# Attention scores in three rounded products from the first pair, an earlier end of the interleaved order, and later front loads

## The chip, the cores and the metric

The kernel runs on one core of a Trainium2 chip. The metric is the time of one execution in microseconds on the device, the median of several runs. The engines are TensorE (PE; PEld are its weight loads), VectorE (DVE), ScalarE (ACT), GpSimd (POOL) and the DMA queues that SyncE (SP) and ScalarE issue.

## What is computed

Block-causal attention over 8 batches, 8 heads, 576 positions of 64 features, and a gated two-layer network on its output.

```python
scores = (1 / sqrt(D)) * q @ k.T              # B, H = 8, 8; S = 576; D = 64
scores = where(row // 64 >= col // 64, scores, -1e9)
attn = softmax(scores)                        # per row, + 1e-9 in the denominator
x = (attn @ v).transpose(0, 2, 1, 3).reshape(4608, 512)
out = (sigmoid(x @ w_gate) * (x @ w_val)) @ w_out    # w_gate, w_val: 512 x 1536, w_out: 1536 x 512
```

Inputs and output are float32, but for the three weight arrays, which arrive as 64-bit numbers and are converted on the chip.

## The kernel before

**Two halves.** The first half goes through 32 pairs of heads (4 pairs a batch): attention, and beside it a first third of the network (`mlp1`, hidden units 0 to 511) for the batch whose four pairs are done. The second half is the rest of the network. The change lies in the first half, roughly the first 580 us of the span.

**Precision.** A matmul takes float32 tiles as they are, in one product, or the kernel rounds a tile to the type F32R (high part H), keeps what rounding left as a second tile (low part L), and adds three products: H with H, L with H, H with L. The network does this throughout (`hidden`, `out_mm`). Attention scores did it only for pairs after `N_FIRST` = 7, and there not for the first 128 rows of q; those, and all scores of pairs 0 to 7, are one float32 product from the tile `KQ` (k and scaled q, transposed).

**A pair.** `prep(p)` makes the transposed tiles. For pairs 0 to 4 PE transposes the loaded rows (`rqk`, two buffers) into PSUM and ScalarE copies them to `KQ` (four copies: k and q, 512 and 64 columns). For pairs 5 to 7 DVE transposes and GpSimd scales q. For pairs 8 on, `split`: DVE transposes, ScalarE rounds K and Q into `KS[0]` and `QS[0]`, DVE subtracts into `KS[1]` and `QS[1]`, GpSimd scales the first 128 columns of q. `QB` holds the last 64 rows of q of both heads side by side for the tail scores. `attend(p)` gives the steps of the pair: "s3", "s2", "sl" (scores and softmax of row blocks 3, 2, and 1 with 0; "s" is all three), "t" (the tail, both heads together), "tr.." (transposes of the probabilities P on PE and their copies G by ScalarE), "r" (`recip`), "AV" (product with v, multiplied by `rb` on DVE, and the output to `X`).

**Reciprocals.** ScalarE sums each row while it computes exponentials, into a column of `sm`: columns 0 to 3 for head 0, 4 to 7 for head 1, column 8 for the tail of both heads (64 partitions each). `recip` inverts, transposes to `rT`, writes `rT` to DRAM (`r_d`, four transfers, L420), and reads it back spread over partitions (`rb`, four transfers, L424). All are on SP's queue.

**Order.** Each pair goes through a list of steps. `FIRST` interleaves the scores of pair p with the transposes of pair p - 1 (capitals: "TR2", "TRt", "TRl", "AV" are of the pair before); `REST` has all scores first and the transposes last; `TURN` is the list in between, for the one pair p = `N_FIRST`. "k" and "q" run `prep(p + 1)` one step further and load k and q of pair p + 3. The number beside a step is how many places it has for matmuls of `mlp1`, twelve a pair; they are dealt evenly (`rate`), tied behind PE instructions of the attention by order edges (`behind`), which also pin the scores in pairs after `N_FIRST` (`rest`, `hold`). Conversions of the weights (`convert`, L85 to L118; fetch on SP, then seven DVE and two ScalarE instructions a piece) are dealt over pairs 0 to 7 by `CONV_PLAN`: w_gate and w_val in pairs 0 to 6, w_out in pairs 5, 6 and 7; a fetch stands behind the last marked instruction of its queue, if there is one. The order on each engine is then fixed by a planner that issues whatever its own model says is ready, the earlier in the code first.

```python
FIRST = (("s3", 1), ("TR2", 1), ("k", 1), ("s2", 1), ("TRt", 1), ("q", 1), ("t", 1), ("TRl", 1), ("sl", 1), ("AV", 2),
         ("tr3", 1), ("r", 0))
REST = (("s", 3), ("t", 1), ("AV", 2), ("tr3", 1), ("r", 0), ("k", 0), ("tr2", 1), ("q", 0), ("trl", 2), ("trt", 2))
for what, places in (FIRST if p < N_FIRST else TURN if p == N_FIRST else REST):
```

The functions that the change touches:

Of the kernel before, what the change touches and what calls it, by code (L numbers as in the profile page):

```python
# [9 lines left out]
F32 = mybir.dt.float32  # L10
F32R = mybir.dt.float32r
# [19 lines left out]
         ("tr3", 1), ("r", 0))  # L31
REST = (("s", 3), ("t", 1), ("AV", 2), ("tr3", 1), ("r", 0), ("k", 0), ("tr2", 1), ("q", 0), ("trl", 2), ("trt", 2))
TURN = (("s3", 1), ("TR2", 1), ("k", 0), ("s2", 1), ("TRt", 1), ("q", 0), ("t", 1), ("TRl", 1), ("sl", 1), ("AV", 1),
        ("tr3", 1), ("r", 0), ("tr2", 1), ("trl", 1), ("trt", 1))
N_FIRST = 7
# [5 lines left out]
def attn_glu_kernel(ctx: ExitStack, tc: tile.TileContext, q, k, v, w_gate, w_val, w_out, out):  # L41
# [119 lines left out]
    with ExitStack() as s2:  # L161
# [9 lines left out]
        KS, QS = [at.tile([P, S], F32R, name=f"K{e}") for e in "HL"], [at.tile([P, S - P], F32R, name=f"Q{e}") for e in "HL"]  # L171
# [16 lines left out]

        QBs = [at.tile([P, 2, D], F32, name=f"QB{i}") for i in range(2)]
        QBS = [at.tile([P, 2, D], F32R, name=f"QB{e}") for e in "HL"]  # L190
        for QB in QBs + [x.bitcast(F32) for x in QBS]:
            nc.gpsimd.memset(QB, 0.0)
# [16 lines left out]
        def load(p, what, queue=nc.sync):  # L209
# [10 lines left out]
            if p <= NP:  # L220

                i, src = (0, k) if what == "k" else (1, q)
                r = rqks[p % 2].rearrange("p i s -> p (i s)").rearrange("p (t c) -> p t c", c=P)
                for h in range(2):
                    queue.dma_start(out=r[:, 4 * i:4 * i + 4, h * D:(h + 1) * D],
                                    in_=src[b, h0 + h, 0:4 * P, :].rearrange("(t p) d -> p t d", p=P))
                queue.dma_start(out=r[64 * i:64 * i + 64, 8, :].rearrange("p (h d) -> p h d", h=2),
                                in_=src[b, h0:h0 + 2, 4 * P:S, :].rearrange("h p d -> p h d"))
                return
# [11 lines left out]
        def mark(engine, ins):  # L241
            last[engine] = ins.ins
# [26 lines left out]
        def prep(p):  # L269

            split = p > N_FIRST
            KQ = cv.tile([P, 2, S], F32, name="KQ", bufs=2)
            QB = QBs[p % 2]

            def transposed(i):
                turn = last.get("DVE")
                mark("DVE", nc.vector.transpose(out=KQ[:, i], in_=rqks[p % 2][:, i]))
                if turn:
                    behind(last["DVE"], turn)

            if p <= NP:

                r = rqks[p % 2].rearrange("p i s -> p (i s)").rearrange("p (t c) -> p t c", c=P)

                def evict(dst, src, i):
                    if i:
                        mark("ACT", nc.scalar.mul(out=dst, in_=src, mul=scale))
                    else:
                        mark("ACT", nc.scalar.copy(out=dst, in_=src))

                for i in range(2):
                    pt = mbank()
                    for t in range(4):
                        transpose(pt[:, t * P:(t + 1) * P], r[:, 4 * i + t], ident)
                    evict(KQ[:, i, :4 * P], pt, i)
                    if i == 0:
                        yield
                pt = mbank()
                transpose(pt[:, :P], r[:, 8], ident)
                for i in range(2):  # L300
                    evict(KQ[:, i, 4 * P:], pt[:, 64 * i:64 * i + 64], i)
                for h in range(2):
                    nc.gpsimd.tensor_copy(out=QB[rows(h), h], in_=KQ[rows(h), 1, S - D:])
                if p == 0:
                    P_first.update({i: p_tile(i) for i in (3, 2, 1, 0, 4)})
                state[p] = KQ, QB, VSs[p % 3]
                yield
                return
            if split:
                transposed(0)  # L310
                transposed(1)
                mark("ACT", nc.scalar.copy(out=KS[0], in_=KQ[:, 0]))
                mark("ACT", nc.scalar.mul(out=QS[0], in_=KQ[:, 1, P:], mul=scale))
                nc.gpsimd.tensor_scalar_mul(KQ[:, 1, :P], KQ[:, 1, :P], scale)
                yield
                mark("DVE", nc.vector.tensor_sub(out=KS[1], in0=KQ[:, 0], in1=KS[0].bitcast(F32)))
                mark("DVE", nc.vector.scalar_tensor_tensor(out=QS[1], in0=KQ[:, 1, P:], scalar=scale,
                                                           in1=QS[0].bitcast(F32), op0=ALU.mult, op1=ALU.subtract))
                for x, src in zip(QBS, QS):
                    for h in range(2):  # L320
                        nc.gpsimd.tensor_copy(out=x[rows(h), h], in_=src[rows(h), S - P - D:])
                state[p] = KQ, QB, VSs[p % 3]
                yield
                return
            for i in range(2):
                transposed(i)
                if i == 1:
                    nc.gpsimd.tensor_scalar_mul(KQ[:, 1], KQ[:, 1], scale)
                    for h in range(2):
                        nc.gpsimd.tensor_copy(out=QB[rows(h), h], in_=KQ[rows(h), 1, S - D:])  # L330
                yield
            state[p] = KQ, QB, VSs[p % 3]

        def attend(p):
            b, hp = pairs[p]
            KQ, QB, VS = state.pop(p)
# [13 lines left out]
            def scores(ps, i, c):  # L350
# [4 lines left out]
                ops = [(KQ[:, 1, q], KQ[:, 0, :n])]  # L355
                if rest and i:
                    q = slice((i - 1) * P, i * P)
                    ops = [(QS[a][:, q], KS[b][:, :n]) for a, b in ((0, 0), (1, 0), (0, 1))]
# [7 lines left out]
            def softmax(ps, i, c):  # L366
# [5 lines left out]
                for h in range(2):  # L372
                    mark("ACT", nc.scalar.activation(out=Pi[:, h], in_=ps[:, h, c:c + n], func=AF.Exp,  # L373
                                                     bias=nm[:, c0 + h:c0 + h + 1], accum_out=sm[:, 4 * h + i:4 * h + i + 1]))
# [21 lines left out]
            def s_tail():  # L396
# [3 lines left out]
                ops = [(QBS[a], KS[b]) for a, b in ((0, 0), (1, 0), (0, 1))] if rest else [(QB, KQ[:, 0])]  # L400
                for half in range(2):
                    for k, (x, y) in enumerate(ops):
# [6 lines left out]
                                                 func=AF.Exp, bias=nm[:, c0:c0 + 1], accum_out=sm[:, 8:9]))  # L409

            def recip():
# [9 lines left out]
                for o, n, src in ((0, 4 * P, r_d[:8].rearrange("(h i) q -> h (i q)", h=2)),  # L421
                                  (4 * P, D, r_d[8].rearrange("(h q) -> h q", h=2))):
                    for h in range(2):
                        nc.sync.dma_start(out=rb[rows(h), o:o + n], in_=src[h].partition_broadcast(D))  # L424
# [328 lines left out]
        for p in range(n + 1):  # L753
# [4 lines left out]
            for what, places in (FIRST if p < N_FIRST else TURN if p == N_FIRST else REST):  # L758
# [8 lines left out]
                elif what in "kq":  # L767
                    next(pr, None)
                    for x in "kq":

                        if p + 3 < n and what == ("q" if p < NP else x):
                            load(p + 3, x)
                elif now:
                    now(what)
# [230 lines left out]
```

## Time and profile before

| | |
|---|---|
| median of three runs | 1217.52 us (1215.24 to 1217.72) |
| the profiled execution | 1215.93 us, span from first to last instruction 1214.1 us |
| PE busy | 1166.7 us, 96% of the span |
| PE weight loads | 1031.1 us, 85% |
| DVE, ACT, POOL busy | 771.9, 626.8, 333.7 us (64, 52, 27%) |
| chain of work that ended last | PE 76%, DVE 13%, DMA 4%, ACT 3% |

Busy PE time is modelled and matmuls overlap, so the distance between the starts of two instructions says more than the length of one. In the chain, a share is the part of the span in which that engine was what everything after it waited for. An average over the span hides that the first 150 us have other limits than the rest, so the stretches are read one by one.

### The profile page before, as it was taken

The numbers are of one execution on the slowest core, as the hardware profiler recorded it, in microseconds if no ns is written. First come the engines' busy times: TensorE is split into PE (matmuls) and PEld (weight loads), VectorE is DVE, ScalarE is ACT, GpSimd is POOL, SyncE is SP. The second block draws the span as 40 slices with busy tenths as digits, with TensorE's granted clock in tenths as the row PEclk, the third lists the DMA queues.
The fourth block names the chain that finished last, engine by engine and source line by source line (L and its number), as shares of the span: only waits on it lengthen the run. The fifth ranks groups of instructions, "written<-read, shape, count | busy, mean of one in ns | idle before, by whom it ended". The sixth has DMA issues, their size and how long they took to land.

```text
span 1214.1 us, 20793 instructions
## 1 busy us (share of the span) xinstructions
PE 1166.7 (96%) x7421; PEld 1031.1 (85%) x7421; DVE 771.9 (64%) x1447; ACT 626.8 (52%) x1447; POOL 333.7 (27%) x411
## 2 busy tenths in 40 slices
PE   6689899999999999999999999999999999999996
PEld 4457688888888888889798899999999998998995
DVE  5676955455463564545799977857867655745743
ACT  6676766666675766666434544444444422422420
POOL 0113232323332332313200133133032162361441
PEclk8899999999999999999999999999999999999998
DMA  8545343534435335444333345145187164263253
GB/s 211 136 120 110 94 113 71 127 67 105 109 79 129 80 85 117 90 103 113 105 106 130 109 148 200 42 159 193 35 307 279 65 201 141 69 208 131 78 156 104
DMA packets 251670, 152.51 MB, mean 126 GB/s; under 512 B 192048, under 2 KB 212528, under 8 KB 250928
## 3 DMA queue, kind: packets, MB, share of 16 engines
q1 hardware_dynamic: 240512, 132.02, 39.0%
q10 hardware_dynamic: 11056, 19.17, 4.4%
q8 instruction: 58, 0.95, 0.3%
q14 instruction: 44, 0.36, 0.1%
HBM read 103.81 MB, written 47.33 MB: 124 GB/s over the span
## 4 chain that ended last, share of the span: by engine, by line
PE 76%; DVE 13%; DMA 4%; ACT 3%; issue 2%; SPq 1%; POOL 1%; POOLq 0%; DVEq 0%; ACTq 0%
PE b L814 22%; PE m L126 14%; PE bank L245 13%; PE m L872 10%; PE m L135 6%; PE bank L248 6%; PE b L872 5%; DVE XL L706 2%; DMA pr<-part_d 1%; ACT P L373 1%; DVE nm L370 1%; DMA raw<-in_moe_w_val_dram 1%; DMA XB<-xT_d 1%; POOL pr L887 1%; DVE cT L616 1%
## 5 line engine op out<-in xcount | busy, mean ns | idle before, releaser
L814 PE MATMUL b<-XH,w 128*128 128x384 f32 x1344 | 351.2, 336 | 4.5 <-DVE g L850 2.0
L814 PEld LDWEIGHTS b<-XH,w 128*128 128x128 f32 x1344 | 244.6, 188 | 10.6 <-DVE v L850 4.5
L814 PE MATMUL b<-XL,w 128*128 128x384 f32 x672 | 225.2, 336 | 0.0
L373 ACT ACTIVATE P<-bank,nm 128x512 f32<-128x512 f32 (+3 forms) x256 | 133.4, 538 | 77.7 <-DVE nm L370 68.9
L814 PEld LDWEIGHTS b<-XL,w 128*128 128x128 f32 x672 | 126.5, 188 | 1.3
L872 PE MATMUL m<-wo,hH 128*128 128x512 f32 x384 | 125.2, 392 | 0.0
L370 DVE TENSOR_REDUCE nm<-bank 128x2 f32<-128x1024 f32 (+3 forms) x128 | 104.9, 820 | 31.4 <-ACT P L373 28.9
L348 ACT COPY G<-bank 128x768 f32<-128x768 f32 (+3 forms) x160 | 106.8, 697 | 34.7 <-PE bank L248 33.5
L126 PE MATMUL m<-XH,wg 128*128 128x288 f32 x448 | 106.3, 307 | 0.0
L126 PE MATMUL m<-XH,wv 128*128 128x288 f32 x448 | 104.6, 304 | 1.7 <-DVE h L147 1.7
L153 POOL TENSOR_TENSOR hL<-h,hH 128x288 fp32r<-128x288 f32 (+1 forms) x56 | 41.9, 749 | 202.1 <-ACT hH L152 191.3
L245 PE MATMUL bank<-G,VS 128*64 128x320 f32 (+4 forms) x896 | 93.9, 360 | 0.3 <-ACT G L348 0.2
L887 POOL TENSOR_TENSOR pr<-pr,pr 128x512 f32<-128x512 f32 x36 | 48.3, 1341 | 160.0 <-DMA pr<-part_d 114.9
L248 PE MATMUL bank<-ident,P 128*128 128x128 f32 x640 | 88.6, 278 | 1.1 <-DVE rT L417 0.6
L245 PEld LDWEIGHTS bank<-G,VS 128*64 128x64 f32 x896 | 55.8, 137 | 36.6 <-issue 1.6
L248 PEld LDWEIGHTS bank<-ident,P 128*128 128x128 f32 x640 | 76.5, 143 | 9.1 <-issue 3.6
L872 PEld LDWEIGHTS m<-wo,hH 128*128 128x128 f32 x384 | 72.2, 188 | 13.7
L705 ACT CAST XH<-XB 128x1536 fp32r<-128x1536 f32 (+2 forms) x72 | 66.1, 938 | 34.2 <-DVE XB L703 25.1
L837 ACT ACTIVATE g<-g 128x384 f32<-128x384 f32 x72 | 37.4, 524 | 82.2 <-DVE g L850 62.1
L126 PEld LDWEIGHTS m<-XH,wg 128*128 128x128 f32 x448 | 75.9, 190 | 3.1 <-issue 1.6
L706 DVE TENSOR_TENSOR XL<-XB,XH 128x1536 fp32r<-128x1536 f32 (+2 forms) x72 | 77.6, 1085 | 1.1 <-ACT XH L705 0.6
L126 PEld LDWEIGHTS m<-XH,wv 128*128 128x128 f32 x448 | 74.7, 188 | 3.8 <-DVE h L147 1.9
(174 smaller groups left out, 2402.6 us busy)
## 6 DMA issues: line engine op xcount, KB each, us to landing
pr<-part_d SPq DMA_DIRECT2D x72, 256.0 KB
xT_d<-xT ACTq DMA_DIRECT2D x32, 288.0 KB
XB<-xT_d SPq DMA_DIRECT2D x16, 576.0 KB
part_d<-ost SPq DMA_DIRECT2D x36, 256.0 KB
out_dram<-ost SPq DMA_DIRECT2D x36, 256.0 KB
VS<-in_v_dram SPq DMA_DIRECT2D x64, 128.0 KB
rb<-r_d SPq DMA_DIRECT2D x64, 128.0 KB
part_d<-ost ACTq DMA_DIRECT2D x32, 256.0 KB
```

The source lines that it names most:

```text
L126: mm = nc.tensor.matmul(ps, lhsT=lh, rhs=rh, start=(i == 0), stop=(i == n - 1))
L135: mm = nc.tensor.matmul(ps, lhsT=lh[:, f, t * P:(t + 1) * P], rhs=rh, start=(i == 0), stop=(i == n - 1))
L245: pe_last[:] = [nc.tensor.matmul(*args, **kw).ins]
L248: pe_last[:] = [nc.tensor.transpose(*args).ins]
L348: mark("ACT", nc.scalar.copy(out=dst, in_=src))
L370: mark("DVE", nc.vector.tensor_reduce(out=nm[:, c0:c0 + 2], in_=ps[:, :, c:c + n], axis=AX.X, op=ALU.max, negate=True))
L373: mark("ACT", nc.scalar.activation(out=Pi[:, h], in_=ps[:, h, c:c + n], func=AF.Exp, bias=nm[:, c0 + h:c0 + h + 1], accum_out=sm[:, 4 * h ...
L705: nc.scalar.copy(out=XO[j][0][:, a:b], in_=x)
L706: sub = nc.vector.tensor_sub(out=XO[j][1][:, a:b], in0=x, in1=XO[j][0][:, a:b].bitcast(F32))
L814: mm = nc.tensor.matmul(ps, lhsT=lh, rhs=rh, start=(first and k == 0), stop=(k == n - 1), skip_group_check=not first)
L872: mm = nc.tensor.matmul(po[t], lhsT=lh[:, f, t * P:(t + 1) * P], rhs=rh, start=(half == 0 and i == 0), stop=(half == 1 and i == 5))
L887: nc.gpsimd.tensor_add(out=pr[0], in0=pr[0], in1=pr[1])
```

## The change

Scores of all pairs, all rows, are three rounded products, from tiles H and L (`KQS`, or for pairs 0, 2 and 4 two buffers of the pool's `KQ`) that hold k and scaled q at full width. For pairs 0 to 4 ScalarE rounds from PSUM into H and DVE subtracts into L; from pair 5 on all pairs are split as pairs 8 on were, with q at full width, and nothing is scaled on GpSimd. `N_FIRST` is 4: pairs 0 to 3 go in `FIRST`, pair 4 in `TURN`, pair 5 on in `REST`. In `FIRST` and `TURN` the loads of pair p + 3 have a step "ld" of their own behind "r"; in `TURN`, "k" and "q" come behind "r" too. The last transfer of each load of the front is marked, so that fetches of conversions stand behind it. The columns of `sm` are laid so that `rb` is read with three transfers.

```diff
 FIRST = (("s3", 1), ("TR2", 1), ("k", 1), ("s2", 1), ("TRt", 1), ("q", 1), ("t", 1), ("TRl", 1), ("sl", 1), ("AV", 2),
-         ("tr3", 1), ("r", 0))
+         ("tr3", 1), ("r", 0), ("ld", 0))
-TURN = (("s3", 1), ("TR2", 1), ("k", 0), ("s2", 1), ("TRt", 1), ("q", 0), ("t", 1), ("TRl", 1), ("sl", 1), ("AV", 1),
-        ("tr3", 1), ("r", 0), ("tr2", 1), ("trl", 1), ("trt", 1))
-N_FIRST = 7
+TURN = (("s3", 1), ("TR2", 1), ("s2", 1), ("TRt", 1), ("t", 1), ("TRl", 1), ("sl", 1), ("AV", 1),
+        ("tr3", 1), ("r", 0), ("k", 0), ("tr2", 1), ("q", 0), ("ld", 0), ("trl", 1), ("trt", 1))
+N_FIRST = 4
...
-        KS, QS = [at.tile([P, S], F32R, name=f"K{e}") for e in "HL"], [at.tile([P, S - P], F32R, name=f"Q{e}") for e in "HL"]
+        KQS = [at.tile([P, 2, S], F32R, name=f"KS{e}") for e in "HL"]
...
-                queue.dma_start(out=r[64 * i:64 * i + 64, 8, :].rearrange("p (h d) -> p h d", h=2),
-                                in_=src[b, h0:h0 + 2, 4 * P:S, :].rearrange("h p d -> p h d"))
+                dma = queue.dma_start(out=r[64 * i:64 * i + 64, 8, :].rearrange("p (h d) -> p h d", h=2),
+                                      in_=src[b, h0:h0 + 2, 4 * P:S, :].rearrange("h p d -> p h d"))
+                if queue is nc.sync:
+                    mark("SP", dma)
...
+            if p <= NP and p % 2 == 0:
+                H, Lo = (cv.tile([P, 2, S], F32R, name="KQ", bufs=2) for _ in "HL")
+            else:
+                H, Lo = KQS
+            state[p] = H, Lo, QBs[p % 2], VSs[p % 3]
+
+            def halves(i, cols, src):
+                if i:
+                    mark("ACT", nc.scalar.mul(out=H[:, 1, cols], in_=src, mul=scale))
+                else:
+                    mark("ACT", nc.scalar.copy(out=H[:, 0, cols], in_=src))
+                yield
+                hi = H[:, i, cols].bitcast(F32)
+                if i:
+                    mark("DVE", nc.vector.scalar_tensor_tensor(out=Lo[:, 1, cols], in0=src, scalar=scale, in1=hi,
+                                                               op0=ALU.mult, op1=ALU.subtract))
+                else:
+                    mark("DVE", nc.vector.tensor_sub(out=Lo[:, 0, cols], in0=src, in1=hi))
...
-                    evict(KQ[:, i, :4 * P], pt, i)
+                    run(halves(i, slice(0, 4 * P), pt))
...
-            for i in range(2):
-                transposed(i)
-                if i == 1:
-                    nc.gpsimd.tensor_scalar_mul(KQ[:, 1], KQ[:, 1], scale)
...
-                ops = [(KQ[:, 1, q], KQ[:, 0, :n])]
-                if rest and i:
-                    q = slice((i - 1) * P, i * P)
-                    ops = [(QS[a][:, q], KS[b][:, :n]) for a, b in ((0, 0), (1, 0), (0, 1))]
+                ops = [(KQ[a][:, 1, q], KQ[b_][:, 0, :n]) for a, b_ in ((0, 0), (1, 0), (0, 1))]
...
-                ops = [(QBS[a], KS[b]) for a, b in ((0, 0), (1, 0), (0, 1))] if rest else [(QB, KQ[:, 0])]
+                ops = [(QB[a], KQ[b_][:, 0]) for a, b_ in ((0, 0), (1, 0), (0, 1))]
...
-                for o, n, src in ((0, 4 * P, r_d[:8].rearrange("(h i) q -> h (i q)", h=2)),
-                                  (4 * P, D, r_d[8].rearrange("(h q) -> h q", h=2))):
-                    for h in range(2):
-                        nc.sync.dma_start(out=rb[rows(h), o:o + n], in_=src[h].partition_broadcast(D))
+                r_f = r_d.rearrange("c q -> (c q)")
+                for h, o, n, f in ((0, 0, S, 0), (1, 4 * P, D, S), (1, 0, 4 * P, S + D)):
+                    nc.sync.dma_start(out=rb[rows(h), o:o + n], in_=r_f[f:f + n].partition_broadcast(D))
...
                 elif what in "kq":
                     next(pr, None)
+                    if p > N_FIRST and p + 3 < n:
+                        load(p + 3, what)
+                elif what == "ld":
                     for x in "kq":
-
-                        if p + 3 < n and what == ("q" if p < NP else x):
-                            load(p + 3, x)
+                        load(p + 3, x)
```

More of the change, by code (lines that the diff above doesn't have):

```diff
@@ L187, in attn_glu_kernel @@
             nc.vector.memset(VS[0:64, 4, :], 0.0)
[L189 to L192, printed above, removed]
+        QBs = [[at.tile([P, 2, D], F32R, name=f"QB{e}{i}") for e in "HL"] for i in range(2)]
+        for QB in QBs[0] + QBs[1]:
+            nc.gpsimd.memset(QB.bitcast(F32), 0.0)
         SMs = [at.tile([P, 32], F32, name=f"sm{i}") for i in range(2)]
@@ L269, in prep @@
         def prep(p):
[L271 to L279, printed above, removed]
+            if p <= NP and p % 2 == 0:
[15 more added lines that the diff above has]
+                    mark("DVE", nc.vector.tensor_sub(out=Lo[:, 0, cols], in0=src, in1=hi))
             if p <= NP:
                 r = rqks[p % 2].rearrange("p i s -> p (i s)").rearrange("p (t c) -> p t c", c=P)
[L285 to L289, printed above, removed]
                 for i in range(2):
@@ L300, in prep @@
                 for i in range(2):
-                    evict(KQ[:, i, 4 * P:], pt[:, 64 * i:64 * i + 64], i)
-                for h in range(2):
[L303 to L319, printed above, removed]
-                    for h in range(2):
[L321 to L324, printed above, removed]
@@ L325, in prep @@
-            for i in range(2):
-                transposed(i)
-                if i == 1:
-                    nc.gpsimd.tensor_scalar_mul(KQ[:, 1], KQ[:, 1], scale)
[L329 to L332, printed above, removed]
+                    run(halves(i, slice(4 * P, S), pt[:, 64 * i:64 * i + 64]))
+            else:
+                KQ = cv.tile([P, 2, S], F32, name="KQ", bufs=2)
+                gens = []
+                for i in range(2):
+                    turn = last.get("DVE")
+                    mark("DVE", nc.vector.transpose(out=KQ[:, i], in_=rqks[p % 2][:, i]))
+                    if turn:
+                        behind(last["DVE"], turn)
+                    gens.append(halves(i, slice(0, S), KQ[:, i]))
+                for x in gens:
+                    next(x)
+                yield
+                for x in gens:
+                    run(x)
@@ L334, in attend @@
+            for QB, x in zip(QBs[p % 2], (H, Lo)):
+                for h in range(2):
+                    nc.gpsimd.tensor_copy(out=QB[rows(h), h], in_=x[rows(h), 1, S - D:])
+            if p == 0:
+                P_first.update({i: p_tile(i) for i in (3, 2, 1, 0, 4)})
+            yield
         def attend(p):
             b, hp = pairs[p]
-            KQ, QB, VS = state.pop(p)
+            H, Lo, QB, VS = state.pop(p)
+            KQ = H, Lo
             G1 = at.tile([P, 2, 1280], F32, name="G1", bufs=1)
@@ L373, in softmax @@
                     mark("ACT", nc.scalar.activation(out=Pi[:, h], in_=ps[:, h, c:c + n], func=AF.Exp,
-                                                     bias=nm[:, c0 + h:c0 + h + 1], accum_out=sm[:, 4 * h + i:4 * h + i + 1]))
+                                                     bias=nm[:, c0 + h:c0 + h + 1], accum_out=sm[:, 5 * h + i:5 * h + i + 1]))
             def s_blocks(*groups):
@@ L408, in s_tail @@
                 mark("ACT", nc.scalar.activation(out=Pt.rearrange("p (a n) -> p a n", a=2), in_=ps[:, :, :288],
-                                                 func=AF.Exp, bias=nm[:, c0:c0 + 1], accum_out=sm[:, 8:9]))
+                                                 func=AF.Exp, bias=nm[:, c0:c0 + 1], accum_out=sm[:, 4:5]))
             def recip():
@@ L420, in recip @@
                     nc.sync.dma_start(out=r_d[:, 32 * j:32 * j + 32], in_=rT[32 * j:32 * j + 9])
-                for o, n, src in ((0, 4 * P, r_d[:8].rearrange("(h i) q -> h (i q)", h=2)),
-                                  (4 * P, D, r_d[8].rearrange("(h q) -> h q", h=2))):
-                    for h in range(2):
-                        nc.sync.dma_start(out=rb[rows(h), o:o + n], in_=src[h].partition_broadcast(D))
+                r_f = r_d.rearrange("c q -> (c q)")
+                for h, o, n, f in ((0, 0, S, 0), (1, 4 * P, D, S), (1, 0, 4 * P, S + D)):
+                    nc.sync.dma_start(out=rb[rows(h), o:o + n], in_=r_f[f:f + n].partition_broadcast(D))
             def tr_main(i):
```

## Prediction

> **What bounds the kernel now.** I read the page's slices first, to see where TensorE (PE) is not the limit, then busy time by stretch of the span, then the order in time of PE, of VectorE (DVE) and of the SyncE queue (SP) through the first pairs.
>
> ```profile
> PE   6689899999999999999999999999999999999996
> PEclk8899999999999999999999999999999999999998
> ```
>
> A slice is 30 us. PE is full from the sixth slice on, so a change to attention pays in two ways only: less PE work in the full slices, or less waiting in the first five. The same by stretch (busy us of PE, PEld, DVE, ACT, POOL, then clock, DMA share, GB/s); the cuts are at the tail scores of a pair (pair 0 to 1, pair 1 to 2, pairs 2 and 3, pair 4 and most of 5, the rest up to pair 8), and the last row is one pair of the steady stage:
>
> ```profile
> 0.00:26.80 26.80, 17.15 (x83) 11.67 (x83) 14.24 (x30) 15.25 (x41) 2.79 (x18) 0.87 0.86 211
> 26.80:46.20 19.40, 12.41 (x82) 7.99 (x82) 10.48 (x21) 10.90 (x31) 1.94 (x3) 0.83 0.64 152
> 46.20:75.00 28.80, 23.65 (x147) 15.20 (x148) 21.03 (x42) 20.95 (x57) 3.90 (x4) 0.88 0.49 116
> 75.00:101.00 26.00, 24.01 (x168) 18.44 (x170) 17.37 (x32) 16.57 (x46) 7.36 (x10) 0.93 0.65 133
> 101.00:147.80 46.80, 42.29 (x316) 33.31 (x312) 42.74 (x81) 33.76 (x86) 13.18 (x17) 1.00 0.43 105
> 170.90:192.00 21.10, 21.10 (x174) 18.56 (x174) 10.56 (x21) 13.33 (x36) 6.16 (x10) 1.00 0.39 97
> ```
>
> Three stages with three limits. Up to 75 us no engine is full and PE stands 21.8 us (9.65 + 6.99 + 5.15): a chain of waits. From 101 to 147.8 DVE is busy 42.74 of 46.8, more than PE. From there on PE is busy all of its time, and DVE half. Pairs 2 and 3 took 14.4 us each, the interval from pair 1 to 2 took 19.4. What sits in those 5 us is the first reciprocal's way through DRAM; rows of SP, DVE and PE in order of time (start, duration):
>
> ```profile
> 21.48 0.98 SPq L87 DMA_DIRECT2D XB<-in_moe_w_out_dram  x2
> 24.03 1.16 SPq L225 DMA_DIRECT2D rqk<-in_k_dram  x2
> 29.52 0.61 SPq L227 DMA_DIRECT2D rqk<-in_q_dram  x1
> 30.22 1.91 SPq L420 DMA_DIRECT2D r_d<-rT  x4
> 32.75 2.58 SPq L234 DMA_DIRECT2D rqk<-in_k_dram  x4
> 35.38 2.42 SPq L424 DMA_DIRECT2D rb<-r_d  x4
> ...
> 25.22 0.19 DVE L417 STREAM_TRANSPOSE rT<-sm 128x32 f32<-128x32 f32 x1
> 39.83 0.82 DVE L468 TENSOR_TENSOR xT<-bank,rb 128x320 f32<-128x320 f32 x2 [5.45 <-DMA rb<-r_d]
> ...
> 29.73 2.93 PE L245 MATMUL bank<-G,VS 128*64 128x320 f32 x28 [0.22 <-ACT G L348]
> 40.71 1.65 PE L245 MATMUL bank<-KQ 64*128 64x384 f32 x4 [4.18 <-DVE xT L468]
> ```
>
> rT is ready at 25.41. SP issues pair 4's loads until 30.13 first, then r_d, then four loads of pair 5, and only then rb. The multiplication that needs rb starts at 39.83, though its product was there at 32.66; DVE stands 5.45 us for it, and PE 4.18 us behind DVE. The loads from 24.03 on are late themselves: pair 5's conversion fetch (XB, issued at 21.48 although its place in the code is pair 5) shares the queue ahead of them while the DMA engines are 0.86 busy.
>
> **The change, part by part.**
>
> *Loads and reciprocal transfers.* Moved: the six k and q loads of pair p+3 from the "q" place to behind "r" for pairs 0 to 4, and, since the last transfer of each load is now the mark that conversion fetches queue behind, those fetches too; one rb transfer of four goes in every pair. From r_d's issue to the multiplication passed 9.61 us, of which pair 5's loads took 2.58. With a free queue that is 7.0: 25.41 + 7.0 = 32.4, about when the product is ready. So the wait goes, and what DVE does next is late for nothing but its own queue. Taken: -5.0, of the ends 0 (the loads stay in front) and -5.45 (the wait itself). The loads come some 5 us later for it; pair 3's are needed for its scores in the third stretch, past 46.2, so they are hidden. The rb transfer less saves SP 0.6 us a pair and is hidden as well: only the first one was waited for.
>
> *Split of K and Q for pairs 0 to 4.* Four DVE subtractions a pair are new, two of 512 columns and two of 64; ScalarE's four copies stay, rounding now.
>
> ```profile
> L118 DVE TENSOR_TENSOR wv<-cgv,wv 128x512 fp32r<-128x512 f32 x4 | 2.7, 685 | 0.2 <-ACT wv L117 0.2
> L316 DVE TENSOR_TENSOR KL<-KQ,KH 128x576 fp32r<-128x576 f32 x1 | 0.7, 729 | 0.0
> 23.53 0.16 DVE L414 TENSOR_SCALAR sm<-sm 128x9 f32<-128x9 f32 x1
> 8.22 0.48 DVE L106 TENSOR_SCALAR cgv<-cgv 128x512 uint32<-128x512 uint32 x1 [6.96 <-DMA cgv<-in_moe_w_gate_dram]
> ```
>
> 2 x 0.685 + 2 x 0.2 (an estimate, just above the 0.16 of nine columns) = 1.77 us a pair. Pair 0's lie in DVE's 6.96 us wait ahead of the first conversion and lengthen it by their end at most: +0.4, between 0 and 1.8. The four of pairs 1 to 4 are 7.1 us; DVE has 7.8 us free in 46.2 to 75 and more before it, but it serves in order and a reduction queues behind them. Ends 0 and 7.1; taken +1.8, a quarter, as ScalarE's copies that release them fall in gaps in which DVE waits for exponentials. Pairs 5 to 7 trade a GpSimd scaling for two subtractions of 576 columns, 1.5 us of DVE each.
>
> *Scores.* One f32 product (before, pairs 0 to 7) against three rounded ones (pairs 8 on, but for the first 128 rows). Starts in order of time; the price of a row is the distance to the next start:
>
> ```profile
> 77.71 0.92 PE L245 MATMUL bank<-KQ 64*128 64x256 f32 x8
> 78.57 0.40 PE L126 MATMUL m<-XL,wg 128*128 128x288 f32 x1
> ...
> 86.22 0.92 PE L245 MATMUL bank<-KQ 64*128 64x384 f32 x4
> 87.07 0.40 PE L126 MATMUL m<-XL,wg 128*128 128x288 f32 x1
> ...
> 111.46 1.21 PE L245 MATMUL bank<-KQ,QB 128*128 128x288 f32 x4 [1.15 <-issue]
> 112.29 0.51 PE L126 MATMUL m<-XH,wv 128*128 128x288 f32 x1
> ...
> 122.28 1.13 PE L245 MATMUL bank<-KQ 64*128 64x512 f32 x4
> 123.34 0.40 PE L126 MATMUL m<-XL,wv 128*128 128x288 f32 x1
> ```
>
> ```profile
> 163.55 0.50 PE L245 MATMUL bank<-KH,QH 64*128 64x512 f32 x2
> 164.37 0.34 PE L245 MATMUL bank<-KH,QH 64*128 64x384 f32 x2
> 164.90 0.28 PE L245 MATMUL bank<-KH,QH 64*128 64x256 f32 x2
> 165.25 0.38 PE L245 MATMUL bank<-KQ 64*128 64x128 f32 x4
> 165.57 0.50 PE L135 MATMUL m<-wo,hL 128*128 128x512 f32 x1
> ...
> 170.94 0.29 PE L245 MATMUL bank<-KH,QBH 128*128 128x288 f32 x1
> 171.07 0.29 PE L245 MATMUL bank<-KH,QBL 128*128 128x288 f32 x1
> ...
> 35.22 0.87 PE L248 MATMUL bank<-ident,P 128*128 128x128 f32 x6
> 35.93 0.60 PE L248 MATMUL m<-ident,rqk 128*128 128x128 f32 x4
> ```
>
> Before: 0.86 + 0.85 + 0.83 + 1.06 = 3.60 us a pair, the first 128 rows (0.32 by the 165.25 row) in the 0.86. In three products: 0.82 + 0.53 + 0.35, and 6 x 0.13 for the tail, = 2.48, and the first rows. These 128-wide rounded products are the one thing the trace never shows. The nearest row is the 256-wide one: six products, two heads at a time, in 0.35. Half the columns can cost half, 0.18; or the weight loads hold them up, and then the upper end is the transposes' row, a load and 128 columns in 0.118, six of them 0.71. The 256-wide row lies nearer (six loads already fit in 0.35), so I take 0.27, the middle of 0.18 and 0.35. A pair then costs 2.75, 0.85 less. In pairs 0 to 3 PE waits anyway: 0. In pairs 8 to 31 PE is full, and only the first rows change: 24 x (0.27 - 0.32) = -1.2, between -3.4 and +9.4. ACT and DVE gain 128 columns each there, hidden by the half of DVE and the third of ACT that are free in the last stretch; the GpSimd scaling that goes was waited for by nobody there.
>
> *Pairs 4 to 7, order ended at pair 4.* PE work falls by 4 x 0.85 = 3.4; PE's idle 2.0 + 4.5 us belongs to the interleaved order's wait at the tail scores and to the turn, and the turn's wait moves to pair 4. Against it DVE gets 3 x 1.5 = 4.5 us, where from 101 us it has 4.1 free in all and the conversions of w_out stay at pairs 5 to 7. Ends: -9.9 (all of PE's saving and idle) and +4.5 (all of DVE's work exposed). Taken -1.0: the saving of pairs 4 and 5, 1.7, less the part of DVE's work that finds no room, 0.7.
>
> Sum: -5.0 + 0.4 + 1.8 - 1.2 - 1.0 = -5.0. The profiled execution took 1215.93 (span 1214.1), so 1210.9 by it; the median of the runs, 1217.52, stands 1.6 higher, so the forecast is **1212.5**. Its own range is 1209 to 1215.5.
>
> **Rivals.**
>
> *Narrow products at the pace of their weight loads (the other side).* Six at 0.118 make the first rows 0.71 instead of 0.27, in the 28 pairs in which PE is full or nearly so: 28 x 0.44 = +12.3, 1224.8. For it: no rounded product under 256 columns stands in the trace, and the transposes show 0.118 at 128. Against it: the six loads of the 256-wide row fit in 0.35. It decides from 0.45 us on, where 28 x 0.18 eats the 5.0.
>
> The Trainium skill, "TensorE: Matmul & The Clock Gate", section "Back-to-back issue gap", gives about 81 ns a matmul for a stream of weight load and 128-wide matmul; by that six would be 0.49 us and the estimate 1212.5 + 28 x 0.22 = 1218.7. The trace speaks against it for products on half the rows: six 256-wide ones took 58 ns each.
>
> *The loads stay in front.* The planner issues what is ready: it put pair 4's loads (24.03 to 29.52) ahead of r_d, though in the code they stand behind it, in pair 1. If it does so again and rb comes as late, the 5.0 is not gained: 1217.5. Against it: the XB fetch and its traffic, now held behind later loads, leave the queue.
>
> *DVE becomes the limit up to pair 8.* All of the 7.1 and 4.5 us shows, against 1.8 and 0.7 counted: +9.1, less the 1.7 to 3.4 that PE no longer needs and that then lies under DVE's time; about 1219. For it: 42.74 of 46.8. Against it: DVE's gaps before 101 us.
>
> *More than counted.* PE's saving is kept whole, half of its idle time goes, DVE's additions hide: -1.8 and -5.6 more, 1205.1.
>
> **How the numbers follow.** Forecast 0.37, narrow products 0.20, loads in front 0.20, DVE 0.13, more than counted 0.10. A measurement of this kernel tells about 0.2%, 2.4 us, from no change. Faster: 0.35 of the forecast, 0.10 of the last, 0.08 of loads and DVE where they are part of the way: 0.53. Same: 0.02 + 0.11 + 0.05 = 0.18. Slower: 0.20 + 0.04 + 0.05 = 0.29. Range 1206 to 1224: it leaves out half of the narrow-product case and of the best one, and takes in the rest.
>
> **What would show it.** Right: r_d issued within a microsecond or two of its rT; no wait for rb before the first L468; the interval from pair 1 to 2 near 14.5 us; the six 128-wide products in under 0.36 us between two starts; pair 8's tail scores some 5 to 6 us earlier than 147.8. Wrong: r_d still behind a row of rqk loads, a start distance of 0.5 us or more at the first rows, or DVE without a gap from pair 4 on and PE waiting for nm. The forecast fails most easily on the narrow products, since 24 of 32 pairs pay them at full price.

## The result, and the profile after

The changed kernel takes 1220.57 us (median of 11 runs, 1219.06 to 1223.78) beside 1217.19 us for the kernel before (11 runs, 1213.26 to 1218.38) on the same chip. The ratio over all runs is 1.0036 with a 95% interval of 1.0023 to 1.0048: slower by 4.4 us (2.8 to 5.8); the two medians alone stand 3.4 us apart. The forecast was 1212.5 us and faster. The profiled execution took 1222.12 us, with a span of 1220.2 us.

The slices of the page after, and the busy time by stretch, cut likewise (us of PE, PEld, DVE, ACT, POOL, then clock, DMA share, GB/s):

```profile
PE   7788899999999999999999999999999999999996
PEclk9898999999999999999999999999999999999999
```

```profile
25.30:40.80 15.50, 13.26 (x100) 9.86 (x101) 11.31 (x25) 10.80 (x31) 3.63 (x9) 0.90 0.70 200
40.80:71.30 30.50, 22.11 (x168) 16.00 (x168) 24.49 (x50) 22.33 (x61) 3.97 (x6) 0.89 0.55 123
97.30:146.80 49.50, 42.69 (x335) 35.85 (x333) 44.18 (x82) 34.55 (x87) 17.44 (x23) 0.93 0.46 109
170.20:191.30 21.10, 21.07 (x174) 18.76 (x174) 11.19 (x22) 14.39 (x38) 4.59 (x9) 1.00 0.39 97
```

The first row, from pair 1's tail scores to pair 2's, is shorter, as forecast (15.5 against 19.4 us). The next, pairs 2 and 3, is longer (30.5 against 28.8), with 24.49 us of VectorE in it instead of 21.03, and the stretch up to pair 8 is longer too (49.5 against 46.8) and at a granted clock of 0.93 instead of 1.00. The last row, a stretch of the steady stage (a little more than pair 9, which takes 18.3 us), looks the same as before. The starts of the tail scores say where the time went (us, read from PE's rows in order of time; the difference is after less before):

```
pair          2      4      5      6      8      9     13     14     16     21     22     24     29     30     31
before    46.24  75.01  90.39 111.46 147.84 170.94 248.50 265.27 299.96 394.95 411.73 446.43 541.42 558.20 574.98
after     40.82  71.28  90.62 108.33 146.76 170.20 248.34 265.77 301.04 396.21 413.63 448.90 544.08 561.50 578.30
difference -5.42  -3.73  +0.23  -3.13  -1.08  -0.74  -0.16  +0.50  +1.08  +1.26  +1.90  +2.47  +2.66  +3.30  +3.32
```

So 5.4 us gained at pair 2 are nearly gone at pair 8, and then comes a loss the prediction did not hold: 4.4 us from pair 8 to pair 31. Most of it, 3.0 us, is in steps of 0.55 to 0.66 us in single pairs, the same ones in every trace that shows them: 13, 15, 21, 23, 29 (pair 31 has one as well, behind its tail scores). Another 0.9 us is lost from pair 8 to 12, and a creep, at most 0.08 us a pair from there on, makes the other 0.5. The step of pair 13 in ScalarE's and TensorE's rows, before and then after (start, duration, engine, line):

```profile
248.26 0.41 ACT L145 ACTIVATE t<-m 128x288 f32<-128x288 f32 x1
248.55 0.59 ACT L373 ACTIVATE P<-bank,nm 128x384 f32<-128x384 f32 x1
249.11 0.60 ACT L373 ACTIVATE P<-bank,nm 128x384 f32<-128x384 f32 x1
...
249.20 0.30 PE L245 MATMUL bank<-KL,QBH 128*128 128x288 f32 x1
249.34 0.29 PE L126 MATMUL m<-XH,wg 128*128 128x288 f32 x1
249.46 0.29 PE L126 MATMUL m<-XL,wg 128*128 128x288 f32 x1
```

```profile
248.06 0.58 ACT L364 ACTIVATE P<-bank,nm 128x384 f32<-128x384 f32 x1
248.62 0.58 ACT L364 ACTIVATE P<-bank,nm 128x384 f32<-128x384 f32 x1
249.18 0.42 ACT L145 ACTIVATE t<-m 128x288 f32<-128x288 f32 x1
...
249.01 0.29 PE L246 MATMUL bank<-KSL,QBH 128*128 128x288 f32 x1
249.65 0.40 PE L126 MATMUL m<-XH,wg 128*128 128x288 f32 x1 [0.34 <-ACT t L145]
249.88 0.30 PE L126 MATMUL m<-XL,wg 128*128 128x288 f32 x1
```

Before, the network's tanh (L145) stands ahead of the two 128x384 exponentials; after, it stands behind them and ends 0.9 us later. The next product into the bank that it reads (L126) waits for it: it starts 0.64 us after the product ahead of it instead of 0.14, and the one behind it follows after 0.23 us instead of 0.12. The code sets no order between the two; the planner chose it. The waits of TensorE from 150 to 590 us, after (total us, times, longest):

```profile
PE m L126 <- ACT t L145: 1.9, 6, 0.4
```

Before has no such row.

The span is longer by 6.1 us, and 3.3 of these have built up at pair 31. The rest comes behind its tail scores: the last group of its products with v starts 19.96 us after them instead of 18.12, with a granted clock of 0.91 in between instead of 1.00. The two other traces with three products everywhere and the order ended at pair 4 show the like (a_unflip 19.81 and a_unhard 19.64 us); b_narrow, with the old end of the order, does not (17.89).

### The profile page after: what moved, and what is told of

The parts are those of the page before. It is cut to its first block, busy times and chain, and to the rows that moved or that the text cites. A ratio compares the mean times of both kernels' runs of the same rounds, so it can differ in the third digit from the quotient of the medians.

```text
span 1220.2 us, 21057 instructions
## 1 busy us (share of the span) xinstructions
PE 1168.5 (96%) x7549; PEld 1039.5 (85%) x7549; DVE 787.1 (65%) x1473; ACT 633.4 (52%) x1453; POOL 320.3 (26%) x400
## 4 chain that ended last, share of the span: by engine, by line
PE 72%; DVE 12%; DMA 5%; ACT 5%; issue 3%; SPq 1%; POOL 1%; ACTq 0%; POOLq 0%; DVEq 0%
PE b L805 22%; PE m L126 11%; PE bank L246 11%; PE m L863 9%; PE m L135 6%; PE bank L249 6%; PE b L863 5%; DMA pr<-part_d 3%; ACT P L364 3%; DVE XL L696 2%; DVE nm L361 1%; POOL pr L878 1%; PE bank L135 1%; PE bank L126 1%; DMA XB<-xT_d 1%
## 5 line engine op out<-in xcount | busy, mean ns | idle before, releaser
L126 PE MATMUL m<-XH,wg 128*128 128x288 f32 x448 | 105.2, 305 | 1.9 <-ACT t L145 1.9
L126 PE MATMUL m<-XH,wv 128*128 128x288 f32 x448 | 103.8, 302 | 1.6 <-DVE h L147 1.6
L246 PE MATMUL bank<-G,VS 128*64 128x320 f32 (+4 forms) x896 | 98.3, 372 | 2.4 <-ACT P L364 2.4
L126 PEld LDWEIGHTS m<-XH,wg 128*128 128x128 f32 x448 | 75.6, 190 | 5.0 <-ACT t L145 3.6
L126 PEld LDWEIGHTS m<-XH,wv 128*128 128x128 f32 x448 | 74.7, 188 | 2.5 <-DVE h L147 1.9
```

What stands on the lines that cost most here:

```text
L126: mm = nc.tensor.matmul(ps, lhsT=lh, rhs=rh, start=(i == 0), stop=(i == n - 1))
L246: pe_last[:] = [nc.tensor.matmul(*args, **kw).ins]
```

## The experiments

Each is timed against the kernel before on the same chip; a gain or loss in us is what the ratio differs from 1, times 1217. A drift is how much later than in the kernel before the tail scores start, compared between two pairs of one trace.

**Order ended at pair 4, alone (b_n4).** The kernel before with one line changed; pairs 5 to 7 thereby get their three products too, but for the first 128 rows.

```diff
-N_FIRST = 7
+N_FIRST = 4
```

> The kernel before with N_FIRST = 4 alone: the turn at pair 4, pairs 5 on in the order with all scores first, split as pairs 8 on were. Theory A (the early end of the interleaved order is what eats the front's gain: with all scores first and the weight conversions still on DVE in pairs 5 to 7, PE runs dry, stands over 2 us at a pair's tail scores and comes back at a lower granted clock): 2 to 4 us slower than before, with idle of over 2 us ahead of the tail scores of pair 6 or 7. Rival B (the order is neutral or a gain, as PE's idle in the interleaved pairs goes, and the loss lies in the steady pairs): same or up to 2 us faster, and the tail scores of pair 8 earlier than 147.8 us.

Measured: 1214.31 us, ratio 0.9985 (0.9971 to 0.9999), -1.8 us. This part gains, by an interval that ends just below no change; the loss is elsewhere. In its trace 0.85 us are lost from pair 8 to 12, without any narrow product: the 0.9 us that the changed kernel loses there go with the end of the order.

**First rows in three products, alone, pairs 8 to 31 (b_narrow).**

```diff
-mark("ACT", nc.scalar.mul(out=QS[0], in_=KQ[:, 1, P:], mul=scale))
-nc.gpsimd.tensor_scalar_mul(KQ[:, 1, :P], KQ[:, 1, :P], scale)
+mark("ACT", nc.scalar.mul(out=QS[0], in_=KQ[:, 1], mul=scale))
...
-                if rest and i:
-                    q = slice((i - 1) * P, i * P)
+                if rest:
```

> The kernel before with the first 128 rows of pairs 8 on in three products too, q split at full width and GpSimd's scaling gone; pairs 0 to 7 as they were. Theory A (the steady stage loses 4 us between the tail scores of pairs 8 and 31: about 0.045 us in each pair for the narrow products, and 0.6 us in five of them where the planner puts ScalarE's tanh behind two exponentials because of the new timings): 1 us slower if the planner keeps its order, 3 to 4 us if it swaps as in the changed kernel. Rival B (drift comes from what the front hands over, such as eight network matmuls dealt earlier): same as before within 0.5 us, no tanh behind exponentials.

Measured: 1221.81 us, ratio 1.0041 (1.0025 to 1.0057), +5.0 us. From pair 8 to pair 31 the tail scores drift by +3.68 us, 3.0 of them in steps in pairs 13, 15, 21, 23 and 29 as in the changed kernel. This part alone loses what the whole change loses. It does not yet say which of its two effects does it, the products or the swap on ScalarE.

**The swap alone (b_flip).** Nothing is computed differently; the tanh is ordered behind the exponentials where the changed kernel has it there.

```diff
+                if i == 2:
+                    exp_last[:] = [last["ACT"]] if p in (13, 15, 21, 23, 29, 31) else []
...
-        nc.scalar.activation(out=t, in_=pg[:, :n], func=AF.Tanh, scale=0.5)
+        tanh = nc.scalar.activation(out=t, in_=pg[:, :n], func=AF.Tanh, scale=0.5)
+        for ins in exp_last:
+            behind(tanh.ins, ins)
```

> The kernel before, nothing computed differently, with edges in the order that put ScalarE's tanh behind the two 128x384 exponentials in pairs 13, 15, 21, 23, 29 and 31, as it stands in the changed kernel; the first rows of pairs 8 on stay in float32. Theory A (the swap itself costs): each of the six pairs gets 0.5 to 0.66 us longer, the tail scores of pair 31 start 3.0 to 3.4 us later than before counted from pair 8, ratio 1.0025 to 1.003. Rival B (the narrow products and the wider copies cost, and the swap is only a sign of it): no step in these pairs, drift under 0.5 us, ratio 1.000.

Measured: the trace drifts by +2.98 us from pair 8 to 31, all of it in the steps, and the span is 2.9 us longer. The wait has appeared in a kernel without any narrow product (TensorE's waits from 150 to 590 us):

```profile
PE m L126 <- ACT t L145: 2.1, 6, 0.4
```

The median moved less than the trace: 1217.37 us, ratio 1.0011 (0.9999 to 1.0024), +1.3 us, with the trace's value at the upper end. In the trace the rival, no step, is excluded; in the medians 2.9 us is only just admitted.

**The swap undone in the changed kernel (a_unflip).**

```diff
+                    if i == 2 and p in (13, 15, 21, 23, 29, 31):
+                        late.append(last["ACT"])
...
+        for ins in late:
+            behind(ins, tanh.ins)
```

> The changed kernel with edges in the order that put the 128x384 exponentials of pairs 13, 15, 21, 23, 29 and 31 behind the tanh again, as in the kernel before; everything else as changed. Theory A: the drift from pair 8 to pair 31 falls from +4.4 to +1.0 us (only the 0.045 us a pair of the narrow products stays), ratio to the kernel before 1.0005 to 1.001. Rival B: the drift stays at +4.4 us and the ratio at 1.0036.

Measured: 1216.43 us, ratio 1.0003 (0.9987 to 1.0019): 4.0 us less than the changed kernel, with an uncertainty of 2.5. The drift from pair 8 to 31 fell from +4.40 to +1.44 us, of which 0.9 are those of pairs 8 to 12, and the row of waits for the tanh is gone. Pair 13's rows now read as before, though the products into it are the split ones:

```profile
244.53 0.41 ACT L145 ACTIVATE t<-m 128x288 f32<-128x288 f32 x1
244.82 0.59 ACT L367 ACTIVATE P<-bank,nm 128x384 f32<-128x384 f32 x1
...
245.46 0.29 PE L249 MATMUL bank<-KSL,QBH 128*128 128x288 f32 x1
245.59 0.29 PE L126 MATMUL m<-XH,wg 128*128 128x288 f32 x1
```

Put in and taken out, the swap moves the trace by 3.0 us both times; that it costs is shown in the traces, and its size in the medians only roughly (1.3 and 4.0 us).

**First rows back in float32 (a_f32first).**

```diff
+                nc.gpsimd.tensor_scalar_mul(KQ[:, 1, :P], KQ[:, 1, :P], scale)
+                first[p] = KQ
...
+                if p in first and i == 0:
+                    ops = [(first[p][:, 1, q], first[p][:, 0, :n])]
```

> The changed kernel with the first 128 rows of the queries back in one float32 product from pair 5 on (GpSimd scales these 128 columns again), the wider copies and the rest as changed. The order on ScalarE is that of the kernel before. Theory A: no steps and no 0.045 us a pair: drift from pair 8 to pair 31 within 0.3 us of the kernel before, ratio 0.9995 to 1.0005. Rival C (a part of the loss is in the first eight pairs or after them, such as the slow stretch around pair 6): ratio above 1.002.

Measured: 1216.97 us, ratio 1.0014 (1.0002 to 1.0025), +1.7 us; from pair 9 to 31 the trace drifts by +0.40 us, and from pair 11 on it stays within 0.2 us. Without narrow products the planner leaves the tanh ahead, and creep and steps are both gone, though the wider copies stay: it is the narrow products that bring the swap, or GpSimd's scaling of these rows that goes with them. The median lies between what the two theories expected. Whether something of the loss is in the front as well is not shown by this run: its one trace stands 0.3 us ahead of the kernel before at pair 31.

**The tanh moved ahead where it is behind before (b_ahead).** As in a_unflip, on the kernel before, for pairs 10, 11, 18 and 26.

> The kernel before with the tanh put ahead of the two 128x384 exponentials in the four pairs where it already stands behind them (10, 11, 18, 26). Theory A says that a tanh behind the exponentials costs only where TensorE waits for what it frees, and the kernel before has no wait of TensorE for a tanh in these pairs: no step, ratio 0.999 to 1.001. Rival (the position behind the exponentials costs 0.5 us wherever it is): four steps of minus 0.5 us, ratio 0.998.

Measured: ratio 1.0007 (0.9992 to 1.0023), and the difference to before is -1.09 us at pairs 9, 10, 11 and 12 alike, and -1.17 at pair 31. No steps: the position costs only where TensorE is waiting for that bank.

**The loads' places alone, as the change puts them (b_ld).** A step "ld" behind "r" issues the loads of pair p+3, and the last transfer of a load becomes SP's mark.

> The kernel before with the loads of pairs 3 to 6 issued from the end of the list and marked, as in the change; nothing else. Theory A (the planner issues what is ready, so this alone leaves the loads of pairs 3 and 4 and the w_out fetch ahead of the first r_d): r_d of pair 0 issued at 28 to 30 us, time within 1 us of before. Rival B (the moved loads are the reason of the 3.3 us by which rb came earlier in the changed kernel): r_d by 27.5, 3 us faster.

Measured: ratio 1.0011 (0.9994 to 1.0027). The planned order of SP still has the loads of pairs 3 and 4 ahead of r_d, which is issued at 27.63 us (30.22 before). The rival expected 3 us, and the wait for rb is still 4.64 us: pair 5's four loads stand between r_d and rb (29.64 to 33.27 us), and from r_d's issue to the multiplication it takes 10.20 us. In SP's rows of the changed kernel r_d is behind eight rows of loads as well, but pair 5's are behind rb; the last row is VectorE's multiplication:

```profile
18.97 1.00 SPq L224 DMA_DIRECT2D rqk<-in_k_dram  x2
...
25.55 0.61 SPq L226 DMA_DIRECT2D rqk<-in_q_dram  x1
26.20 1.07 SPq L87 DMA_DIRECT2D XB<-in_moe_w_out_dram  x2
27.36 1.39 SPq L411 DMA_DIRECT2D r_d<-rT  x4
...
32.37 1.77 SPq L414 DMA_DIRECT2D rb<-r_d  x3
...
36.56 0.82 DVE L458 TENSOR_TENSOR xT<-bank,rb 128x320 f32<-128x320 f32 x2 [1.28 <-DMA rb<-r_d]
```

What went behind pair 4's loads in both is the conversion fetch XB (26.20 instead of 21.48 in the changed kernel, 26.46 in b_ld); in the changed kernel the loads are through by 26.16 instead of 30.13, and r_d is issued 2.9 us earlier (2.6 in b_ld).

**The loads really behind (b_ldhard).** b_ld with order edges.

```diff
+                    if last_r:
+                        behind(first.ins, last_r[0])
...
+                        last_r[:] = [nc.sync.dma_start(out=rb[rows(h), o:o + n], in_=src[h].partition_broadcast(D)).ins]
```

> The kernel before with order edges that do force the loads of pairs 3 to 6 behind the rb transfers of pairs 0 to 3, and the fetches of conversions behind those loads; nothing else. Theory A (the first wait for rb is a real 5 us on the path, and PE is full from pair 8 on, so what the front saves is kept): r_d of pair 0 within 1 us of rT (25.4 us), no idle of DVE for rb, tail scores of pair 2 some 5 us earlier, the whole 4 to 5 us faster than before. Rival B (the time is given back in pairs 4 to 8, where DVE's conversions set the pace, or the later loads make new waits): tail scores of pair 4 earlier but those of pair 8 not, time same.

Measured: ratio 0.9986 (0.9972 to 0.9999), -1.7 us. r_d is issued as rT is done (23.57 and 23.54 us), but VectorE still waits 2.71 us for rb, since from r_d to the multiplication it takes 9.23 us. Pair 2 is 6.4 us earlier, pair 4 2.7, pair 8 1.0, pair 9 0.5 us later. The 5 us exist and do not last. Of the 6.9 us given back from pair 2 to pair 9, 4.5 go in pairs 3, 4 and 8. There TensorE has as many products as before (74, 97 and 153) and stands as long to 0.1 us, but at a lower granted clock (us from a pair's tail scores to the next pair's, us of it in which TensorE stands, granted clock):

```
                  pair 3              pair 4              pair 8
before       14.34 2.77 0.90     15.38 1.98 1.00     23.10 0.00 1.00
b_ldhard     15.68 2.67 0.80     17.02 1.99 0.90     24.64 0.00 0.93
```

What lowers the clock is not shown. The loads' places are not needed for it: in b_flip pair 4 took 16.97 us at 0.90, with the loads and the early order of the kernel before.

**Both in the changed kernel (a_unhard).** a_unflip with these edges.

> a_unflip with edges that force the loads of pairs 3 to 7 behind the spread of the reciprocals of the pair in which they are issued: the loads really go behind, which the change's marks did not bring about. Theory D (the front's gain is given back by pair 9, as when the edges were put into the kernel before): pairs 1 and 2 come 5 to 6 us earlier, pair 9 about 0 to 1 us, ratio 1.7 us below a_unflip's, about 0.9995. Rival, the prediction's own step: the 5 us stay to the end, ratio about 0.997.

Measured: ratio 1.0019 (1.0005 to 1.0033), +2.3 us, no better than a_unflip (1.9 us above it, with an uncertainty of 2.6). Its trace is 5.0 us ahead of the kernel before at pair 2 and 1.8 at pair 9, where a_unflip's is 6.9 and 4.3 us ahead. The prediction's 5 us are not there even with the loads where the prediction wanted them.

**The split of the first pairs in the old order (a_split8).** a_f32first with the order of steps, the loads and N_FIRST = 7 of the kernel before. From pair 5 on there is one set of rounded halves, and with the interleaved order kept to pair 7, the next pair's rounding overwrites it between the score blocks: in pairs 5 to 7 later blocks are computed from the next pair's halves.

> The kernel before in its order of steps, loads and end of the interleaved order, with the split of the scores into three products in the first eight pairs alone taken over from the change (pairs from 9 on keep float32 first rows). Theory E (the split of the first eight pairs costs nothing on the path beyond what the prediction put, +0.4 us for the front and +1.8 us by pair 8): tail scores of pair 8 later by 2 us at most, no drift after pair 8, ratio 1.000 to 1.002. Rival F (VectorE's subtractions become the limit up to pair 8): pair 8 later by 4 us or more, ratio above 1.003. Rival G (three products at the full rate beat one in float32, pairs 1 to 7 shorter): pair 8 earlier, ratio below 0.999.

Measured: ratio 1.0074 (1.0056 to 1.0093), +9.0 us. It does not price the split, since most of its loss comes from that overlap: in pairs 5 and 6 TensorE stands for the next pair's rounding (2.23 and 6.80 us; its rows in order of time):

```profile
90.34 0.45 PE L246 MATMUL bank<-KSH 64*128 64x384 f32 x2 [2.23 <-ACT KSH L281]
...
114.47 0.69 PE L246 MATMUL bank<-KSH 64*128 64x384 f32 x2 [6.80 <-ACT KSH L281]
```

It shows why the split and the earlier end of the interleaved order go together in the change.

**The two parts that gained, together (b_n4hard).** b_ldhard with N_FIRST = 4 and no new split.

> The two parts that each came out slightly faster, together and without any new split: the interleaved order ends at pair 4, and the loads of pairs 3 to 6 are forced behind the spread of the reciprocals. If the two add up: ratio 0.997 (1.8 and 1.7 us). If both only remove the same slack in pairs 2 to 9: ratio 0.9985. The order on ScalarE in pairs 13 to 31 is that of the kernel before, so no drift after pair 9.

Measured: 1210.43 us beside 1215.36, ratio 0.9954 (0.9938 to 0.9969), -5.6 us. More than the sum of the two (3.5), which the intervals admit. It is the fastest of all and beats both kernels.

**The split of pairs 0 to 4 on top of that (a_f32hard).** a_f32first with the load edges. Beside the split it differs from b_n4hard in that "k" and "q" of pair 4 stand behind "r", the rounding of q is 576 wide, and one rb transfer a pair is gone.

> The changed kernel with the first 128 rows back in float32 from pair 5 on (as in a_f32first: no swap on ScalarE, no narrow products there) and the loads of pairs 3 to 7 forced behind the spread of the reciprocals. Against b_n4hard (0.9954) it differs mainly in that pairs 0 to 4 are split into three products. Theory H (that split costs what the front gains, through the extra roundings on ScalarE and subtractions on VectorE ahead of each pair's scores): ratio 1.000 to 1.001, that is 5 to 6 us above b_n4hard, lost between pairs 0 and 9. Rival (the split of pairs 0 to 4 is free and the differences between the kernels so far are chance): ratio 0.995 to 0.997. The term of the prediction, 2.2 us for the split of the front: ratio 0.997 to 0.998.

Measured: 1216.57 us, ratio 1.0005 (0.9990 to 1.0021): 6.2 us above b_n4hard, with an uncertainty of 2.7. The busy time from the start to the tail scores of pairs 3, 5 and 8, b_n4hard and then a_f32hard (columns as above):

```profile
0.00:57.54 57.54, 40.41 (x238) 26.71 (x239) 36.54 (x72) 37.89 (x102) 7.68 (x24) 0.90 0.62 147
57.54:90.43 32.89, 30.21 (x202) 22.72 (x202) 23.12 (x46) 22.32 (x58) 5.59 (x7) 0.86 0.62 135
90.43:143.32 52.89, 46.28 (x385) 39.83 (x384) 48.41 (x92) 39.57 (x105) 21.08 (x27) 1.00 0.54 137
```

```profile
0.00:56.91 56.91, 41.38 (x272) 30.59 (x273) 39.73 (x86) 36.85 (x97) 9.33 (x30) 0.88 0.61 146
56.91:95.00 38.09, 31.26 (x219) 24.20 (x219) 26.44 (x52) 24.53 (x62) 7.28 (x11) 0.82 0.53 124
95.00:149.53 54.53, 47.73 (x384) 40.35 (x384) 45.96 (x90) 39.73 (x104) 20.06 (x27) 0.97 0.58 135
```

In these two traces the kernels are level at pair 3, 4.6 us apart at pair 5, 6.2 at pair 8, and 4.5 at pair 9, since b_n4hard's pair 8 ran at a lower clock (0.93 against 1.00). So no loss has come of the split up to pair 3, though VectorE has 3.2 us more in the first stretch. In the middle stretch it has 3.3 us more, and TensorE stands 6.8 us instead of 2.7, but the granted clock is lower too (0.82 against 0.86), so the 4.6 us are not all the split's. A part of them is the turn at pair 4: the roundings of pair 5's k and q stood at 73.42 and 74.15 us in b_n4hard, 11 us ahead of their scores; here they stand at 86.24 and 88.75, and TensorE waits for the second:

```profile
73.42 0.69 ACT L319 CAST KH<-KQ 128x576 fp32r<-128x576 f32 x1
74.15 0.60 ACT L320 ACTIVATE QH<-KQ 128x448 fp32r<-128x448 f32 x1
...
85.87 0.50 PE L252 MATMUL bank<-KH,QH 64*128 64x512 f32 x2
```

```profile
86.24 0.67 ACT L288 CAST KSH<-KQ 128x576 fp32r<-128x576 f32 x1
88.75 0.70 ACT L286 ACTIVATE KSH<-KQ 128x576 fp32r<-128x576 f32 x1
...
89.51 1.03 PE L251 MATMUL bank<-KSH 64*128 64x512 f32 x6 [1.54 <-ACT KSH L286]
```

## Why the prediction was wrong, step by step

*Scores in pairs 8 to 31 (-1.2): wrong in sign, the step that failed most.* The price of the six narrow products was taken as 0.27 us between 0.18 and 0.35. It is just outside, 0.38 from 103.35 to the next start at 103.73, and 0.37 to 0.42 in the steady pairs:

```profile
103.35 0.23 PE L246 MATMUL bank<-KSH 64*128 64x128 f32 x2
103.41 0.28 PE L246 MATMUL bank<-KSH,KSL 64*128 64x128 f32 x2
103.53 0.27 PE L246 MATMUL bank<-KSL,KSH 64*128 64x128 f32 x2
103.73 0.40 PE L126 MATMUL m<-XH,wv 128*128 128x288 f32 x1
```

The first two pairs of products go at the rate of half the columns (0.06 and 0.12 us), but the last pair holds up the next instruction for 0.20. Against the 0.32 of the float32 product the six are 0.06 us a pair dearer by these rows; the traces show less, 0.5 us of creep from pair 12 to 31. The Trainium skill, "TensorE: Matmul & The Clock Gate", "Back-to-back issue gap", gives about 81 ns a product of 128 columns with its weight load; the six took 63 ns each, so the trace does not bear it out here. The larger part, 3.0 us in the traces of b_flip and a_unflip, was in no term and no rival: the work did not only change its length, it changed what the planner put first on ScalarE, in six pairs in which TensorE waits for it. That nobody waited for GpSimd's scaling was right (TensorE's waits before, from 150 to 590 us, name no GpSimd); what moved in its place was not looked for. The rival of the narrow products named the right place with the wrong mechanism: it needed 0.45 us and got 0.38.

*Loads and reciprocal transfers (-5.0).* The premise failed, and so did the conclusion, separately. The loads of pairs 3 and 4 did not go behind r_d, as the second rival said; yet the wait for rb fell from 5.45 to 1.28 us and the interval from pair 1 to 2 to 15.5 us, near the 14.5 named. That nearness is partly luck. The multiplication came 3.27 us earlier, 2.86 of them because XB went behind pair 4's loads and r_d was issued earlier; the other 0.9 us of the wait is time that VectorE spent on the new subtractions ahead of it. The 7.0 us from r_d to the multiplication, worked out by taking off the 2.58 of pair 5's loads, did not come: with these loads behind rb it took 9.20 us, after 9.61. It was 7.44 in a_unhard. The sign named for this step, r_d issued within a microsecond or two of its rT, held (27.36 after 26.13 us) with the loads still in front, so it did not tell the forecast from its rival. And the gain does not reach the end: the edges that force the move gave 6.4 us at pair 2 and 1.7 over the timed runs. The prediction carried a wait's length from pair 2 to the last pair without asking what pairs 3 to 9 would make of it; in b_ldhard's trace 4.5 us went in three of these pairs at a lower granted clock, a term that the prediction did not have.

*Split of K and Q (+0.4 and +1.8).* Too small, as far as a_f32hard tells. The upper end was 7.1 us; a_f32hard shows 6.2 (3.5 to 8.9) above b_n4hard, with the turn's change and whatever the clock did in it. In the changed kernel as it stands less of it can show: the narrow part with its swap takes 4.4 to 5.0 us of its loss and the order's end gives 1.8 back, so that, if the parts add up, the split and the loads together are left with 1 to 2 us.

*Pairs 4 to 7 (-1.0).* Held for what b_n4 contains of it, -1.8 (-3.5 to -0.1). "The turn's wait moves to pair 4" was named without a price; it is the 1.54 us above.

*VectorE as the limit up to pair 8.* Not shown. It is busy 44.18 of 49.5 us, more than TensorE, as it was before. That the measured time lies near this rival's 1219, and inside the range, is luck: b_narrow, which leaves pairs 0 to 7 as they were, loses as much as the whole change.

Not settled: what lowers the granted clock in the front, and which of a_f32hard's differences from b_n4hard carries how much. That the front's gains shrink from pair 8 to 9 (2.0 us in b_n4hard, 1.5 in b_ldhard) goes with the clock, 0.93 in both; in b_n4, whose pair 8 has the same 146 products as b_n4hard's, it was 1.00 and the pair 1.65 us shorter.

## What to carry to other kernels

In a kernel whose order a planner sets, a change of a few hundredths of a microsecond on one engine can reorder another engine; compare the order of every engine at the steady stage before pricing the change, and pin the order where a busy engine waits for it. A wait removed early is worth only what the stages behind it leave of it, so follow it pair by pair to the last, with the granted clock beside each pair. And a change of several parts is worth taking apart: here the earlier end of the order and the loads, forced behind by edges, gained 5.6 us together, while the whole change lost 4.4.

## What the runs showed of the hardware

TensorE's granted clock fell after a pause of 2 us in one trace and not in another. In a_unflip TensorE stood 2.23 us ahead of 104.99; from 105.53 on a product's row is 0.44 us long instead of 0.29, and from 104.99 to 112.60 us, with another pause of 0.77 us in it, the clock was 0.55, and 28 products took 5.36 us. In b_n4hard, after pauses of 2.41 and 0.77 us at the same place of the kernel, it stayed at 1.00, and 28 of them took 2.93:

```profile
105.53 0.44 PE L249 MATMUL bank<-KSH,QBH 128*128 128x288 f32 x1
...
107.22 5.36 PE L249 MATMUL bank<-G,VS 128*64 128x320 f32 x28 [0.77 <-ACT P L367]
...
104.99:112.60 7.61, 6.84 (x35) 0.55 0.23 73
```

```profile
110.61 2.93 PE L252 MATMUL bank<-G,VS 128*64 128x320 f32 x28 [0.77 <-ACT P L380]
...
108.81:113.50 4.69, 3.92 (x35) 1.00 0.42 119
```

The front also differs between traces of the same order: the changed kernel and a_unflip issue the same instructions in the same order up to pair 13, and their tail scores of pair 8 start at 146.76 and 143.18 us. Their pair 4 took 19.34 us at a granted clock of 0.91 and 17.77 at 1.00. One trace tells the steady stage to a tenth of a microsecond and the front to some 3 us, so the worth of the parts in the front is judged here by medians, and the traces only say where the time went.
